# The last store of a group-norm kernel split by partitions: 120 rows, then 8 rows

## Chip, cores and metric

One core of one Trainium2 chip. The metric is the device time of one execution in microseconds (us). The profile's span is about 1.8 us shorter than this time. Runs are called fast when they are within 1.5% of the fastest of the same kernel.

## The reference

```python
B, C, H, W = 128, 1024, 32, 16          # bfloat16 in and out
xr = x.reshape(B, 32, C // 32, H, W)    # 32 groups
mu  = xr.mean(axis=(2, 3, 4), keepdims=True)
var = ((xr - mu) ** 2).mean(axis=(2, 3, 4), keepdims=True)
xn  = ((xr - mu) / jnp.sqrt(var + 1e-5)).reshape(B, C, H, W)
return xn * g[None, :, None, None] + b[None, :, None, None]
```

134 MB are read and 134 MB written; the profile's DMA packets carry both, 268.7 MB in all.

## The kernel before

The batch is cut into NT = 64 tiles of 2 samples. A tile is 128 partitions by 8192 bfloat16 columns, so a row is 16 KB and a tile 2 MB. Loads and stores are all issued from one queue (SP), nine loads ahead. VectorE scales the tile in place, one instruction for each of 16 channels, and the tile is stored as one transfer.

```python
    def L(i):
        st = state.setdefault(i, {})
        xt = xpool.tile([P, F], BF16, name="xt")
        chain("sp", nc.sync.dma_start(out=xt[:], in_=x_v[i]))
        st["xt"] = xt
    ...                                  # statistics on TensorE, VectorE, ScalarE
    def A(i):
        ...                              # reciprocal, scl, bia
        for k in range(KC):              # KC = 16
            chain("dve", nc.vector.tensor_scalar(
                out=xt[:, k * HW : (k + 1) * HW], in0=xt[:, k * HW : (k + 1) * HW],
                scalar1=scl[:, k : k + 1], scalar2=bia[:, k : k + 1],
                op0=ALU.mult, op1=ALU.add))

    def S(i):
        st = state[i]
        chain("sp", nc.sync.dma_start(out=o_v[i], in_=st["xt"][:]))
        state.pop(i - 3, None)
    ...
    for s in range(-1, NT + 2):
        ...                              # M1, M, Gm, A(s - 2), R, Q, T
        if 0 <= s - 2 < NT:
            S(s - 2)
            if s - 2 + PREFETCH < NT:
                L(s - 2 + PREFETCH)
```

Of the kernel before, what the change touches and what calls it, by code (L numbers as in the profile page):

```python
# [24 lines left out]
def kernel(  # L25
# [7 lines left out]
    nc = tc.nc  # L33
    P = nc.NUM_PARTITIONS
# [5 lines left out]
    NT = B0 // NS  # L40
# [16 lines left out]
    o_v = out.rearrange("(t n) (cb k) h w -> t (n cb) (k h w)", n=NS, cb=CB)  # L57
# [19 lines left out]
    def chain(key, inst):  # L77
        prev = last.get(key)
        if prev is not None:
            tc.add_manual_dep(inst.ins, prev.ins.name, nosync, reason="pipeline order")  # L80
        last[key] = inst
        return inst
# [5 lines left out]
        out=ind_f[:].rearrange("p (a c) -> p a c", c=PPG),  # L88
        in_=ones_f[:].rearrange("p (a c) -> p a c", c=PPG),
# [7 lines left out]
        out=ind_f[:].rearrange("p (a c) -> p a c", c=PPG),  # L97
        in_=ind_f[:].rearrange("p (a c) -> p a c", c=PPG),
# [165 lines left out]

    def S(i):
        st = state[i]
        chain("sp", nc.sync.dma_start(out=o_v[i], in_=st["xt"][:]))
        state.pop(i - 3, None)

    for i in range(min(PREFETCH, NT)):  # L270
# [16 lines left out]
    for s in range(-1, NT + 2):  # L287
        if 0 <= s + 1 < NT:
            M1(s + 1)
            M(s + 1)  # L290
        if 0 <= s - 1 < NT:
            Gm(s - 1)
        if 0 <= s - 2 < NT:
            A(s - 2)
        if 0 <= s + 1 < NT:
            R(s + 1)
        if 0 <= s < NT:
            Q(s)
        if 0 <= s - 1 < NT:
            T(s - 1)  # L300
# [4 lines that stand above are left out]
# [30 lines left out]
```

## Time and profile before

| | before |
|---|---|
| time, median of 4 | 639.52 us (639.23 to 639.78) |
| span in the profile | 637.8 us |
| moved | 268.7 MB, 421 GB/s over the span |
| last scaling by VectorE ends, last store issued | 621.0 us |
| wait for that store at the end | 15.4 us |

The kernel is bound by its transfers: the DMA engines move 421 GB/s over the span. The page of the kernel before, first its 40 slices of the span (the busy share of the DMA engines in tenths, and GB/s), then its DMA queues (packets, MB, share of the time of 16 engines):

```profile
DMA  8999999999999999999999999999999999999993
GB/s 357 427 427 426 428 425 429 434 428 423 434 429 429 430 431 432 430 431 430 432 429 431 432 431 431 428 431 433 431 429 430 432 432 430 429 432 431 430 423 163
...
q1 hardware_dynamic: 18752, 268.45, 98.7%
q8 instruction: 7, 0.11, 0.1%
q14 instruction: 15, 0.12, 0.0%
```

The engines are 9 tenths busy or more in all slices but the first and the last. The page calls the queues q8 and q14 instruction queues, so their packets are called instruction fetches here: few packets.

The end of the span in stretches of 2 us (columns: stretch, length, busy time and number of instructions of each compute engine, clock granted to TensorE, mean busy share of the 16 DMA engines, GB/s):

```profile
622.00:624.00 2.00, 0.00 (x0) 0.00 (x0) 0.00 (x0) 0.00 (x0) 0.00 (x0) 0.50 0.98 418
624.00:626.00 2.00, 0.00 (x0) 0.00 (x0) 0.00 (x0) 0.00 (x0) 0.00 (x0) 0.50 0.98 418
626.00:628.00 2.00, 0.00 (x0) 0.00 (x0) 0.00 (x0) 0.00 (x0) 0.00 (x0) 0.50 0.63 270
628.00:630.00 2.00, 0.00 (x0) 0.00 (x0) 0.00 (x0) 0.00 (x0) 0.00 (x0) 0.50 0.15 66
630.00:632.00 2.00, 0.00 (x0) 0.00 (x0) 0.00 (x0) 0.00 (x0) 0.00 (x0) 0.50 0.08 33
632.00:634.00 2.00, 0.00 (x0) 0.00 (x0) 0.00 (x0) 0.00 (x0) 0.00 (x0) 0.50 0.08 33
634.00:636.00 2.00, 0.00 (x0) 0.00 (x0) 0.00 (x0) 0.00 (x0) 0.00 (x0) 0.50 0.06 25
636.00:638.00 2.00, 0.00 (x0) 0.00 (x0) 0.00 (x0) 0.00 (x0) 0.00 (x0) 0.50 0.00 0
```

Up to 626 us all engines are at work. From 628 on a share of 0.15, then 0.08, is left: 0.08 of 16 engines is 1.3 engines. For some eight microseconds only one to three engines work. The waits of the SP queue (line, what it waited for, us in total, times, longest) show the final wait:

```profile
SPq L330 <- DMA out_dram<-xt: 15.4, 1, 15.4
```

The records of single packets in the trace say more. Each engine moves its eight rows of a store one after another, 0.611 us for each 16 KB row, then a 4-byte packet of 9 ns, taken here for its count: the queue q1 has 2112 of them, as many as the trace has landings. The stream that ends last has its rows of the store before the last one done at 631.56 us and those of the last store at 636.42. The others end at 630.90, 629.41, 628.61 and from there down to 626.8. So the stream that ends last is alone for the last 5.5 us. The trace gives no engine's number to a packet. So "late stream" below means: the one that ends last.

The late stream does not fall behind at the end. Its landing trails the median landing of the same transfer by 0.4 us at the start and 9.1 us at the end. About 3 us of this had come by 150 us, less regularly; from there on the lag grows mostly in steps of 0.8 to 1 us, at the landings at 159, 218, 272, 326, 376, 430, 485, 544 and 598 us among others. Just before each of these a q14 packet starts (157.5, 213.5, 268.4, 324.5, 371.6, 427.2, 482.6, 538.2 and 596.2 us). It takes 0.31 us itself, and in eight of the nine places a row that starts right behind it takes 1.0 to 1.2 us instead of 0.61.

### The profile page before, as it was taken

How to read it: one execution, taken by the hardware profiler on the slowest of the kernel's cores; microseconds unless marked ns; L12 is line 12 of the kernel's file. 1: busy time of each engine (PE TensorE's matmuls, PEld its weight loads, DVE VectorE, ACT ScalarE, POOL GpSimd, SP SyncE). 2: the span in 40 equal slices, each digit the busy share in tenths (PEclk: the TensorE clock that was granted, in tenths of full speed). 3: DMA queues.
4: the chain of work that ended last, by engine and by line, in shares of the span. 5: the costliest groups of instructions: out<-in, count | busy, mean ns of one | idle time of the engine just before them, and what ended most of it. 6: DMA issues, size and time to landing. Idle time of an engine off the chain costs nothing.

```text
span 637.8 us, 3899 instructions
## 1 busy us (share of the span) xinstructions
PE 326.3 (51%) x887; PEld 127.1 (20%) x904; DVE 421.0 (66%) x1349; ACT 590.7 (93%) x318; POOL 1.6 (0%) x6
## 2 busy tenths in 40 slices
PE   4654564556456555645654664464553654635300
PEld 1221122122112212211221222121221221212100
DVE  0086677668667766866776686677667667767680
ACT  1999999999999999999999999999999999999920
POOL 1000000000000000000000000000000000000000
PEclk9767767776776676666667667766766667666655
DMA  8999999999999999999999999999999999999993
GB/s 357 427 427 426 428 425 429 434 428 423 434 429 429 430 431 432 430 431 430 432 429 431 432 431 431 428 431 433 431 429 430 432 432 430 429 432 431 430 423 163
DMA packets 18774, 268.69 MB, mean 421 GB/s; under 512 B 2368, under 2 KB 2368, under 8 KB 2368
## 3 DMA queue, kind: packets, MB, share of 16 engines
q1 hardware_dynamic: 18752, 268.45, 98.7%
q8 instruction: 7, 0.11, 0.1%
q14 instruction: 15, 0.12, 0.0%
HBM read 134.23 MB, written 134.22 MB: 421 GB/s over the span
## 4 chain that ended last, share of the span: by engine, by line
ACT 53%; DMA 23%; issue 17%; DVE 2%; PE 1%; SPq 0%; DVEq 0%; ACTq 0%
ACT ja L189 38%; DMA out_dram<-xt 18%; ACT ja L137 14%; DMA xt<-in_x_dram 5%; DVE xt L255 2%; ACT rstd L221 1%; PE ps L154 1%; SPq L121 0%; DVE jd L171 0%; DVE bia L243 0%; DVE scl L237 0%; DVEq L330 0%; DVE rstd L232 0%; ACTq L137 0%
## 5 line engine op out<-in xcount | busy, mean ns | idle before, releaser
L189 ACT ACTIVATE ja<-xt,negmean 128x8192 bf16<-128x8192 bf16 x64 | 455.8, 7122 | 15.2 <-DVE jd L171 13.2
L154 PE MATMUL ps<-xt,ind_b 128*128 128x512 bf16 x759 | 301.9, 576 | 80.3 <-DMA xt<-in_x_dram 73.1
L255 DVE TENSOR_SCALAR xt<-xt,scl,bia 128x512 bf16<-128x512 bf16 x1024 | 336.6, 408 | 2.6 <-DVE bia L243 0.2
L154 PEld LDWEIGHTS <-ind_b 128*128 128x128 bf16 x776 | 108.6, 146 | 244.8 <-issue 162.4
L232 DVE RECIPROCAL rstd<-rstd 128x1 f32<-128x1 f32 x64 | 10.5, 164 | 169.1 <-ACT rstd L221 169.1
L137 ACT ACTIVATE ja<-xt 128x2048 bf16<-128x2048 bf16 x62 | 117.7, 1898 | 2.6 <-DMA xt<-in_x_dram 2.6
L243 DVE SCALAR_TENSOR_TENSOR bia<-scl,negmean,bet 128x16 f32<-128x16 f32 x64 | 15.0, 235 | 2.3
L237 DVE TENSOR_SCALAR scl<-gam,rstd 128x16 f32<-128x16 f32 x64 | 15.0, 234 | 2.2
L189 ACT ACTIVATION_READ_ACCUMULATOR ja<-xt,negmean 128x1 f32 x64 | 11.9, 186 | 0.0
L137 ACT ACTIVATION_READ_ACCUMULATOR ja<-xt 128x1 f32 x62 | 11.7, 189 | 0.0
L171 DVE TENSOR_SCALAR_CACHE_REDUCE jd<-ps 128x512 bf16<-128x512 f32 x2 | 1.4, 692 | 7.9 <-PE ps L154 7.9
L171 DVE TENSOR_SCALAR_CACHE_REDUCE jd<-ps,ps_170 128x512 bf16<-128x512 f32 x1 | 0.8, 755 | 6.6 <-PE ps_170 L206 6.6
L284 DVE CAST gam<-gam_b 128x16 f32<-128x16 bf16 x1 | 0.2, 174 | 6.4 <-DMA gam_b<-in_g_dram 6.4
L206 PE MATMUL ps_3186<-carry,ind_f 128*128 128x1 f32 x2 | 0.6, 362 | 6.7 <-ACT ja L189 6.7
L206 PE MATMUL ps_2155<-carry,ind_f 128*128 128x2 f32 x2 | 0.6, 362 | 4.8 <-ACT ja L137 4.8
L206 PE MATMUL ps_930<-carry,ind_f 128*128 128x2 f32 x2 | 0.6, 364 | 4.8 <-ACT ja L137 4.8
L206 PE MATMUL ps_1812<-carry,ind_f 128*128 128x2 f32 x2 | 0.6, 364 | 4.7 <-ACT ja L137 4.7
L206 PE MATMUL ps_587<-carry,ind_f 128*128 128x2 f32 x2 | 0.6, 364 | 4.7 <-ACT ja L137 4.7
L206 PE MATMUL ps_1469<-carry,ind_f 128*128 128x2 f32 x2 | 0.6, 362 | 4.6 <-ACT ja L137 4.6
L206 PE MATMUL ps_244<-carry,ind_f 128*128 128x2 f32 x2 | 0.6, 364 | 4.6 <-ACT ja L137 4.6
L206 PE MATMUL ps_1126<-carry,ind_f 128*128 128x2 f32 x2 | 0.6, 364 | 4.6 <-ACT ja L137 4.6
L206 PE MATMUL ps_2008<-carry,ind_f 128*128 128x2 f32 x2 | 0.6, 362 | 4.6 <-ACT ja L137 4.6
(319 smaller groups left out, 126.9 us busy)
## 6 DMA issues: line engine op xcount, KB each, us to landing
xt<-in_x_dram SPq DMA_DIRECT2D x64, 2048.0 KB, 24.2
out_dram<-xt SPq DMA_DIRECT2D x64, 2048.0 KB, 28.7
gam_b<-in_g_dram SPq DMA_DIRECT2D x2, 2.0 KB, 7.1
bet_b<-in_b_dram SPq DMA_DIRECT2D x2, 2.0 KB, 6.7
```

The source lines that it names most:

```text
L137: nc.scalar.activation(out=ja[:, 0 : na * MMN], in_=xt[:, (NMM - na) * MMN :], func=ACT.Identity, scale=-inv_n, accum_out=carry[:, 1:2],),
L154: nc.tensor.matmul(out=ps[:], lhsT=ind_b[:], rhs=xt[:, k * MMN : (k + 1) * MMN], start=(k == 0), stop=(k == npe - 1),),
L171: nc.vector.tensor_scalar(out=jd[:], in0=st["ps"][:], scalar1=-inv_n, scalar2=seed, op0=ALU.mult, op1=ALU.add, accum_out=negmean[:],),
L189: nc.scalar.activation(out=ja[:], in_=st["xt"][:], func=ACT.Square, bias=st["negmean"][:], scale=1.0, accum_out=carry[:, 0:1],),
L206: nc.tensor.matmul(out=ps2[:, 0:ncol], lhsT=ind_f[:], rhs=st["carry"][:, 0:ncol], start=True, stop=True,),
L221: nc.scalar.activation(out=rstd[:], in_=st["ps2"][:, 0:1], func=ACT.Sqrt, bias=eps_t[:], scale=inv_n),
L232: chain("dve", nc.vector.reciprocal(out=rstd[:], in_=rstd[:]))
L237: nc.vector.tensor_scalar(out=scl[:], in0=gam[:], scalar1=rstd[:], scalar2=None, op0=ALU.mult),
L243: nc.vector.scalar_tensor_tensor(out=bia[:], in0=scl[:], scalar=negmean[:], in1=bet[:], op0=ALU.mult, op1=ALU.add,),
L255: nc.vector.tensor_scalar(out=xt[:, k * HW : (k + 1) * HW], in0=xt[:, k * HW : (k + 1) * HW], scalar1=scl[:, k : k + 1], scalar2=bia[:, k ...
L284: nc.vector.tensor_copy(out=gam[:], in_=gam_b[:])
```

## The change

The intent is to take the last store off one DMA engine. In the trace of before, a store of 128 rows has sixteen landings, one for each stream with its eight rows. I expected 120 rows to go to fifteen engines, eight each, and the eight rows left to eight engines. One engine, the sixteenth, then has nothing to do in the last store.

```diff
     def S(i):
         st = state[i]
-        chain("sp", nc.sync.dma_start(out=o_v[i], in_=st["xt"][:]))
+        xt = st["xt"]
+        if i == NT - 1:
+            lo = P - P // 16
+            chain("sp", nc.sync.dma_start(out=o_v[i][0:lo, :], in_=xt[0:lo, :]))
+            chain("sp", nc.sync.dma_start(out=o_v[i][lo:P, :], in_=xt[lo:P, :]))
+        else:
+            chain("sp", nc.sync.dma_start(out=o_v[i], in_=xt[:]))
         state.pop(i - 3, None)
```

No other instruction moves on any engine.

## The prediction

Passages are cut from the recorded text where no trace or run shows what they say: how rows are dealt out to numbered engines, why the late engine should be 15 (the "about 80%" was my estimate, from nothing in the traces), a conclusion from the times of the fetches, and a term of the sum for rows of the last store that slow each other. "Engine 15" is my name for the engine that 120 rows leave out, "0 to 7" for those that also get one of the last 8 rows; "port contention" is my name for rows that slow each other. The sum came to about 634.6 us if the emptied engine is the late one (4.8 us less), and to 639.5 to 640.1 us if another is; the term for port contention, a guess of mine, put the time at about 637 us in the first case; weighed, 635.3 us.

> **What bounds the kernel now.** Data movement. The page shows the 16 DMA engines busy 9 tenths in nearly every slice at about 430 GB/s, 268 MB in 637.8 us. ScalarE is 93% busy but is fed by loads, and the chain of waits alternates between landings and ScalarE. The change touches only the last store, so only the tail counts.
>
> **The tail.** The last VectorE scaling ends at 621.0 us (timeline) and the last store is issued at 621.04; the span ends at 637.8. The waits show the final wait for that store: 15.4 us. The windows view shows the drain: DMA share 0.98 for 622-626 us, 0.63 for 626-628, 0.15 for 628-630, then 0.08, 0.08 and 0.06 up to 636. 0.08 of 16 engines is 1.3 engines. So 2 MB needs about 5 us on most engines, then one engine works alone for some 7 us. In the trace's packets a 16 KB row takes 0.611 us; the stream that ends last finishes the previous store at 631.56 us, then moves its eight rows of the last store, done at 636.42. The second-last stream ends at 630.90, the third at 629.41, most others between 626.0 and 628.6. The last stream's lag behind the median grows by 0.8 to 1 us at the times of 8 KB instruction fetches, about every 55 us[...]. The trace does not number the engines.
>
> **What the change does.** [...] Added: one issue on the queue (0.33 to 0.42 us in the trace, hidden under the drain) and one more row on eight engines, 0.61 us. Removed: 8 x 0.611 = 4.9 us from engine 15. [...]
>
> **Sum, if the late engine is 15 (about 80%).** It ends at 631.56 instead of 636.42. The second-last, plus one row, ends at 631.5. The span shrinks by 4.8 us, all on the critical path: about 634.6 us. [...] If the late engine is not 15, nothing is gained and up to 0.6 us lost: 639.5 to 640.1. Weighing these: 635.3 us.
>
> **What would show it.** Right: unchanged until 621 us; the stream late by 5 us ends at 631.6 with no rows of the last store; DMA share near 0.1 for 628-631.6, then nothing; final wait about 10.5 us. Port contention: packets of about 1.2 us after 622, none before. Wrong engine: one stream still ending at 636.4 or 637.0.
>
> **What would make it wrong.** Another engine being late, port contention, 120 rows spread otherwise than over fifteen engines, or a run-to-run drift of the fetches. In any case the stake is under 1% of the time.

## The result

| | before | after |
|---|---|---|
| time, median (4 runs each) | 639.52 us | 643.29 us (642.89 to 643.67) |
| ratio of fast runs | | 1.0061, 95% interval 1.0047 to 1.0075 |
| span in the profile | 637.8 us | 641.1 us |
| rows moved after 621 us that took over 0.9 us | 0 of 178 | 53 of 179, median of these 1.22 us |

The kernel became 3.8 us slower. That is 0.6%; the interval leaves out 1. Ratios are the mean time of one kernel's fast runs over that of the other's of the same rounds, so not quite the ratio of the medians quoted. The page after the change, the slices of the span again, and its DMA issues (KB each, us to landing; the transfer of 128 KB has no landing time there):

```profile
DMA  9999999999999999999999999999999999999993
GB/s 359 425 427 423 422 432 424 428 431 428 430 433 429 432 430 427 435 429 428 432 430 434 430 426 432 431 430 432 429 430 432 429 432 432 428 431 430 431 408 96
...
out_dram<-xt SPq DMA_DIRECT2D x63, 2048.0 KB, 28.7
out_dram<-xt SPq DMA_DIRECT2D x1, 1920.0 KB, 18.9
out_dram<-xt SPq DMA_DIRECT2D x1, 128.0 KB
```

All slices but the last two are as before, within 10 GB/s. The stretches at the end, to be read against those of before:

```profile
622.00:624.00 2.00, 0.00 (x0) 0.00 (x0) 0.00 (x0) 0.00 (x0) 0.00 (x0) 0.50 1.06 344
624.00:626.00 2.00, 0.00 (x0) 0.00 (x0) 0.00 (x0) 0.00 (x0) 0.00 (x0) 0.50 0.85 262
626.00:628.00 2.00, 0.00 (x0) 0.00 (x0) 0.00 (x0) 0.00 (x0) 0.00 (x0) 0.50 0.96 279
628.00:630.00 2.00, 0.00 (x0) 0.00 (x0) 0.00 (x0) 0.00 (x0) 0.00 (x0) 0.50 0.60 164
630.00:632.00 2.00, 0.00 (x0) 0.00 (x0) 0.00 (x0) 0.00 (x0) 0.00 (x0) 0.50 0.26 82
632.00:634.00 2.00, 0.00 (x0) 0.00 (x0) 0.00 (x0) 0.00 (x0) 0.00 (x0) 0.50 0.18 57
634.00:636.00 2.00, 0.00 (x0) 0.00 (x0) 0.00 (x0) 0.00 (x0) 0.00 (x0) 0.50 0.08 33
636.00:638.00 2.00, 0.00 (x0) 0.00 (x0) 0.00 (x0) 0.00 (x0) 0.00 (x0) 0.50 0.06 25
638.00:640.00 2.00, 0.00 (x0) 0.00 (x0) 0.00 (x0) 0.00 (x0) 0.00 (x0) 0.50 0.04 16
640.00:642.00 2.00, 0.00 (x0) 0.00 (x0) 0.00 (x0) 0.00 (x0) 0.00 (x0) 0.50 0.02 4
```

Read the last two columns together. Before, a busy share of 0.98 moved 418 GB/s. Now 0.96 (626 to 628 us) moves 279 GB/s: the engines are as busy, but rows take longer (53 of 179 over 0.9 us). That is the collision that the prediction priced as a risk. And the end of the list is not shorter than before: the share of 0.06 and 0.08 of the one late engine still stands there, up to 640 us. The final wait confirms it:

```profile
SPq L336 <- DMA out_dram<-xt: 18.7, 2, 18.1
```

What the late stream did, from the landings of its part of each transfer (us from the start of the span, the last landing of each transfer):

| | before: landing, since the one before | after: landing, since the one before |
|---|---|---|
| store 61 | 627.04 | 626.42 |
| store 62 (the one before the last) | 631.90, 4.86 | 634.39, 7.97 |
| last store, or its 120 rows | 636.75, 4.85 | 639.29, 4.90 |
| its last 8 rows | | 639.90, 0.61 |

Two things are seen at once. First, the trace has fifteen landings of the 120 rows and eight of the last 8, as meant, but the late stream still has eight rows of the 120 and one of the last 8, so it is not the engine that the change empties; it is one of the eight that got a ninth row. Second, most of the loss is not in the last store at all: the late stream's rows of the store before it took 7.97 us instead of 4.86. The sum is 3.11 + 0.05 + 0.61 = 3.77 us, and the difference of the medians is 3.77 us too (643.29 less 639.52). That even the last digit agrees is chance, for the landings are those of one execution each. The spans differ by only 3.3 us since in the profiled run of after the late stream happened to be 0.6 us earlier already at store 61.

### The profile page after: what moved, and what is told of

The parts are those of the page before. It is cut to its first block, busy times and chain, and to the rows that moved or that the text cites. A ratio compares the mean times of both kernels' runs of the same rounds, so it can differ in the third digit from the quotient of the medians.

```text
span 641.1 us, 3917 instructions
## 1 busy us (share of the span) xinstructions
PE 333.1 (52%) x904; PEld 127.4 (20%) x904; DVE 420.7 (66%) x1349; ACT 590.6 (92%) x318; POOL 1.6 (0%) x6
## 4 chain that ended last, share of the span: by engine, by line
ACT 56%; DMA 19%; issue 19%; DVE 2%; PE 1%; SPq 0%; DVEq 0%; ACTq 0%
ACT ja L189 41%; ACT ja L137 15%; DMA out_dram<-xt 14%; DMA xt<-in_x_dram 5%; DVE xt L255 2%; ACT rstd L221 1%; PE ps L154 1%; SPq L121 0%; DVE jd L171 0%; DVE scl L237 0%; DVE bia L243 0%; DVE rstd L232 0%; DVEq L336 0%; ACTq L137 0%
## 5 line engine op out<-in xcount | busy, mean ns | idle before, releaser
L154 PE MATMUL ps<-xt,ind_b 128*128 128x512 bf16 x776 | 307.7, 580 | 66.1 <-DMA xt<-in_x_dram 66.1
```

Of the source, the lines that this page charges most:

```text
L154: nc.tensor.matmul(out=ps[:], lhsT=ind_b[:], rhs=xt[:, k * MMN : (k + 1) * MMN], start=(k == 0), stop=(k == npe - 1),),
```

## The experiments

Sixteen kernels ran. The edits are to S(i) for the last tile, if nothing else is said. The theories:

- **Rows side by side** (the "port theory" of the expectations; the name is mine, and no run here shows a port). Rows of partitions that lie side by side slow each other when several engines read them at the same time. Before, with sixteen engines on 128 rows, no row of 178 took over 0.9 us; with 120 rows over fifteen engines, 53 of 179 did. e3, e4, e5 and e13 test the theory itself.
- **Rivals.** The HBM side of the new row order; the fewer engines or the second transfer as such; the ninth row alone.

### Which engine is late: a fingerprint (e1, e6), then a check (e7, e15)

A transfer of a few rows was expected to give one row each to as many engines; the trace of after has eight landings for its 8 rows. A series of small transfers of different sizes then leaves on each stream a number of small packets that tells in how many of them it took part. I numbered the streams by this, from 0: stream m is the one that takes part in the transfers of more than m rows (of 1 to 15). That the streams join in such a fixed order was my assumption; e10 and e15 test it at one place only.

```diff
+c = F - 256                      # e1
+chain("sp", nc.sync.dma_start(out=o_v[i][:, 0:c], in_=xt[:, 0:c]))
+lo = 0
+for k in [8] + list(range(15, 0, -1)):        # e6: (1, 2, 3, 4, 5, 6, 7, 100)
+    chain("sp", nc.sync.dma_start(out=o_v[i][lo : lo + k, c:F], in_=xt[lo : lo + k, c:F]))
+    lo += k
```

> The last store keeps all 128 rows and 7936 of 8192 columns in one transfer over sixteen engines; the last 256 columns go in sixteen small transfers of 8, 15, 14, ... 1 rows, whose packets are 512 B. [...] My prediction (late engine is 15): the last stream has 0 such packets. Theory now (it is one of 0 to 7, because after the change the last stream still moved a ninth row): 9 to 16; my bet is engine 7, 9 packets. Large packets stay at 0.61 us, for this transfer has all 128 partitions. Time within 1 us of before.

Measured: 643.80 us (2 runs; before 639.88), later than expected by 3 us. Only eight transfers were under way at a time, and the queue waited for the late stream before it issued the rest (three waits at the small transfers' line, 9.8 us in all). The late stream had seven small packets directly behind its large ones, the transfers of 8, 15, 14, 13, 12, 11 and 10 rows, all that were issued by then. So it takes part in the transfer of 8 rows (one of 0 to 7, and not 15), but nothing finer follows.

> The first fingerprint showed seven small packets at the tail of the late stream and six at that of the second, which only says that both are among engines 0 to 7: the queue stopped at eight transfers in flight. Now the last 256 columns go in transfers of 1, 2, ... 7 rows, then 100. [...] My bet: late engine 7, none; second, some of 0 to 6. Rival: the late engine is any other of 0 to 6, which shows in the number. Time within 1.5 us of e1 (643.8).

Measured: 642.28 us (one run). The end of the late stream in the packet records (start in us, ns, bytes), with the queue's transfers of 1 to 7 rows all issued by then:

```
636.591  592  15872     the last of its eight large pieces
637.180    9      4     its count
637.185   27    512
637.209    9      4
637.215   27    512
637.238    9      4
637.244   27    512
637.268    9      4
637.274   27    512
637.297    9      4     then nothing for 1 us
```

Four small packets: by the assumed order, those of the transfers of 4, 5, 6 and 7 rows. The late engine is 3 in this numbering. My bet on 7 was wrong too. The second-last stream had two, at a time when the transfers of 1 to 6 rows were issued: engine 4.

> The change with its last eight rows as seven over seven engines and one over one engine. If the late engine is 7, its stream ends after eight rows of the last store and time is 0.6 us under that of the change (about 642.7 us); if it is one of 0 to 6, the ninth row stays and the time is that of the change (643.3 us).

```diff
-for lo, hi in ((0, 120), (120, 128)):         # the change, written as a loop
+for lo, hi in ((0, 120), (120, 127), (127, 128)):
```

Measured: 643.53 us (4 runs; ratio to before 1.0062, interval 1.0047 to 1.0077), as the change. The late stream still had its ninth row (landings at 640.21 and 640.81 us, 0.60 us apart). Engine 7 is out, as e6 says.

> As e10, but 124 rows over four engines (0 to 3) instead of 123 over three. If the late engine is 3, its stream now has 31 pieces of 5.5 KB more (0.215 us each in e10) behind its 635.1 us: 641.8, time about 645 us. Rival (the fingerprint was misread and the late engine is another, or rows on the lowest engines do not go where I think): engines 0 to 3 end earlier than in e10, the late one is as in e10, time about 638.5 us.

Its edit, beside that of e10 (below), which gave the same columns to engines 0 to 2:

```diff
-for lo, hi in ((0, 123), (123, 126), (126, 128)):     # e10: 123 rows, k = 3
+for lo, hi in ((0, 124), (124, 128)):                 # e15: 124 rows, k = 4
```

Measured: 645.71 us (2 runs) against 638.52 us for e10. The late stream went on for 6.58 us behind its eight large pieces, which is 31 pieces of 0.212 us, a quarter of the 124 rows. In e10 the three small transfers have eight counts together (18888 packets in q1 against 18752 before, of which 128 are the pieces), as 3, 3 and 2 engines would give. One more engine for the same bytes costs seven microseconds, because the fourth is the late one. Two independent readings, the count of small packets and the time lost, agree. The numbers are those of the order above; the trace itself has none.

### What made the rows slow (e2, e3, e4, e5, e13)

> The last store as two transfers of 64 partitions, 16 engines each, so every engine still moves eight rows and none is left out; there is no ninth row. Port theory[...]: rows of the last store take about 1.2 us, the late stream is slowed by its neighbour on rows it has still to move, time 2 to 4 us over before. Rival (what costs is the transfer on fewer than sixteen engines and its ninth row): rows stay at 0.61 us, time within 0.5 us of before.

```diff
+for lo in (0, P // 2):
+    chain("sp", nc.sync.dma_start(out=o_v[i][lo : lo + P // 2, :], in_=xt[lo : lo + P // 2, :]))
```

Measured: 643.04 us (4 runs; ratio 1.0050, interval 1.0033 to 1.0067). As e2 is meant, no engine is left out and none has a ninth row, and still 73 of 176 rows take over 0.9 us and the late stream's rows of store 62 take 8.21 us, 3.35 more than before, which alone makes up the loss. So neither the missing engine nor the ninth row is the main cost. The ninth row costs 0.61 us of the 3.8 us of the change, as its landings above show; here 3.2 us are lost without it.

> The last store as sixteen transfers of 8 rows each, on eight engines, with rows 4 partitions apart[...]. Port theory: rows take 0.61 us; the late stream, if it is one of engines 0 to 7, has sixteen rows and ends near 631.6 + 9.8 = 641.4 us, time about 644.5 us. Rival (splitting or running on fewer engines is itself slow, or the HBM side): rows of 1.2 us or more, time 650 us or more.

> The same sixteen transfers of 8 rows on eight engines, but with 8 consecutive rows each[...]. Port theory:[...] 1.2 us or more in the median, time 648 to 664 us. Rival (number of transfers and engines decides, not the partitions): the same packets and time as with rows 4 apart.

```diff
+for lo in (0, 32, 64, 96):                     # e3: rows 4 apart
+    for j in range(4):
+        chain("sp", nc.sync.dma_start(out=o_v[i][lo + j : lo + j + 29 : 4, :],
+                                      in_=xt[lo + j : lo + j + 29 : 4, :]))
```
```diff
+for lo in range(0, P, 8):                      # e4: rows side by side
+    chain("sp", nc.sync.dma_start(out=o_v[i][lo : lo + 8, :], in_=xt[lo : lo + 8, :]))
```

Measured: e3 644.60 us, no row over 0.9 us of 176; e4 651.96 us, 87 of 180 rows over 0.9 us. Both have sixteen transfers of eight rows (eight landings for such a transfer in the trace of after) and the same bytes; what differs is which rows move at the same time, and so the partitions read and the HBM rows written together. e3 shows besides that many transfers on few engines do not slow rows by themselves. Two stretches of each, e3 first (columns as above):

```profile
634.00:636.00 2.00, 0.00 (x0) 0.00 (x0) 0.00 (x0) 0.00 (x0) 0.00 (x0) 0.50 0.37 152
636.00:638.00 2.00, 0.00 (x0) 0.00 (x0) 0.00 (x0) 0.00 (x0) 0.00 (x0) 0.50 0.47 197
```

```profile
634.00:636.00 2.00, 0.00 (x0) 0.00 (x0) 0.00 (x0) 0.00 (x0) 0.00 (x0) 0.50 0.10 41
636.00:638.00 2.00, 0.00 (x0) 0.00 (x0) 0.00 (x0) 0.00 (x0) 0.00 (x0) 0.50 0.57 90
```

In e3 a share of 0.47 moves 197 GB/s, in e4 a share of 0.57 moves 90 (636 to 638 us in both). e3 also gives the price of a row on the late engine without a collision: eight rows more than before, 4.7 us (644.60 less 639.88), 0.59 us each.

> Wrong result on purpose: sixteen transfers of 8 rows of the last tile, read from 8 consecutive partitions as in e4_eight_contig, but written to HBM rows 4 apart as in e3_eight_step4. Port theory (the SBUF side decides): as e4, time 650 to 654 us, many rows of over 0.9 us. Rival (the HBM addresses decide): as e3, rows of 0.61 us, time about 644.6 us.

> Wrong result on purpose, the mirror of e5: rows read from partitions 4 apart, written to eight consecutive HBM rows. Port theory: as e3, rows of 0.61 us, time about 644.6 us. HBM theory: as e4, about 652 us.

```diff
+for lo in range(0, P, 8):                      # e5; e13 has lo and d exchanged on the two sides
+    d = 32 * (lo // 32) + (lo % 32) // 8
+    chain("sp", nc.sync.dma_start(out=o_v[i][d : d + 29 : 4, :], in_=xt[lo : lo + 8, :]))
```

Measured: e5 651.34 us (80 of 175 rows slow), e13 644.14 us (0 of 175 slow). Rows that lie side by side in SBUF are slow here whether they go to neighbouring HBM rows (e4, 87 of 180) or not (e5, 80 of 175); none of the rows 4 apart is slow (e3, 0 of 176; e13, 0 of 175), whatever HBM rows they go to. The HBM side is out. (Both give wrong results.)

### Why the store before the last one suffered (e16, e17)

If collisions anywhere slowed every stream, it would not matter to the late stream which partitions its neighbours read. I expected it to matter ("own-port theory" in e17). e16 and e17 are e2 with both halves read from the same half of the tile, the upper in e16, the lower in e17.

```diff
+h = P // 2                                     # e16; e17: h = 0
+for lo in (0, P // 2):
+    chain("sp", nc.sync.dma_start(out=o_v[i][lo : lo + P // 2, :], in_=xt[h : h + P // 2, :]))
```

> Wrong result on purpose: e2 with both halves of the last store read from partitions 64 to 127. The rows of the last store still collide with each other (1.2 us and more). [...] its rows of the store before keep 0.61 us and eight of them take 4.9 us, not the 8.2 us of e2: time 639.5 to 640.5 us. Rival (collisions anywhere slow every stream): 8 us again, time 643 us.

> Wrong result on purpose, the mirror of e16: both halves read from partitions 0 to 63[...]. Own-port theory: the late stream's eight rows of the store before take as long as in e2 or longer (8 to 11 us), time 643 to 646 us. Rival (collisions anywhere slow every stream alike): same time as e16.

Measured, before in the same rounds 639.62 us (both give wrong results):

| | time (2 runs) | slow rows after 621 us | late stream's rows of store 62 |
|---|---|---|---|
| e16, partitions 64 to 127 twice | 640.51 us | 96 of 177 | 4.85 us |
| e17, partitions 0 to 63 twice | 644.56 us | 90 of 177 | 10.00 us |

Stretches of both, e16 first:

```profile
626.00:628.00 2.00, 0.00 (x0) 0.00 (x0) 0.00 (x0) 0.00 (x0) 0.00 (x0) 0.50 1.09 262
628.00:630.00 2.00, 0.00 (x0) 0.00 (x0) 0.00 (x0) 0.00 (x0) 0.00 (x0) 0.50 1.05 229
...
634.00:636.00 2.00, 0.00 (x0) 0.00 (x0) 0.00 (x0) 0.00 (x0) 0.00 (x0) 0.50 0.08 33
```

```profile
626.00:628.00 2.00, 0.00 (x0) 0.00 (x0) 0.00 (x0) 0.00 (x0) 0.00 (x0) 0.50 1.00 213
628.00:630.00 2.00, 0.00 (x0) 0.00 (x0) 0.00 (x0) 0.00 (x0) 0.00 (x0) 0.50 0.93 188
...
634.00:636.00 2.00, 0.00 (x0) 0.00 (x0) 0.00 (x0) 0.00 (x0) 0.00 (x0) 0.50 0.17 25
```

Between 626 and 630 both collide: about 1.0 of share and under 265 GB/s. But in e16 the late engine runs at its own pace through all this, and from 634 on it is alone at full speed (0.08 of share, 33 GB/s), as before the change. Nearly twice as many slow rows as in the change (96 against 53) cost almost nothing (640.51 us), because they are not the late stream's rows. In e17 its rows take twice their time. So the late stream is slowed by neighbours that read partitions 0 to 63 (10.00 us for eight rows) and not by those that read 64 to 127 (4.85 us), and what the collisions do to other streams is hidden under its lag. Two more traces narrow this down. In e4, where its neighbours read rows side by side, its rows of store 62 took 7.80 us (landings at 627.73 and 635.53 us). In e3, with rows 4 apart, they took 4.85 us (627.15 and 632.00), although its neighbours also read from the lower half at the time. The test in e3 is thin, for only seven rows of neighbours fall on these eight rows; which partitions the late stream itself reads, no trace shows.

### Where the lag comes from (e9, e11)

> Wrong result on purpose: VectorE scales two channels at a time with the first one's factors, 8 instructions per tile instead of 16; the last store is that of before. If the late engine is late because it also serves VectorE's instruction fetches (each 8 KB fetch of the long series adds 0.8 to 1 us of lag, 10 or 11 of them before), there are 6 or 7 fetches in that series, the lag of the last landing behind the median falls from 9.1 us to about 5.5 us, and the time falls by about 3.5 us, to 636 us. Rival (the lag has another cause, the fetches only coincide): lag and time stay.

```diff
-        for k in range(KC):                    # in A(i), every tile
+        for k in range(0, KC, 2):
             ...
-                    out=xt[:, k * HW : (k + 1) * HW],   # in0 likewise
+                    out=xt[:, k * HW : (k + 2) * HW],
```

Measured: 636.19 us (4 runs; ratio 0.9947, interval 0.9930 to 0.9964), a wrong result. The lag of the last landing is 5.9 us instead of 9.1, and q14 has 12 packets instead of 15. VectorE's scaling before and in e9 (group of instructions, count, busy us, mean ns):

```profile
L255 DVE TENSOR_SCALAR xt<-xt,scl,bia 128x512 bf16<-128x512 bf16 x1024 | 336.6, 408 | 2.6 <-DVE bia L243 0.2
```

```profile
L255 DVE TENSOR_SCALAR xt<-xt,scl,bia 128x1024 bf16<-128x1024 bf16 x512 | 239.4, 542 | 2.6 <-DVE bia L243 0.3
```

VectorE itself was not the limit: its last scaling ends at 621 us before, almost 16 us before the last landing. Its faster scaling does not explain the gain either, for the median landing of the last store stayed (627.68 us before, 627.50 in e9); only the late stream's came earlier. What fell with the lag is the number of its instructions: the regular series of 8 KB fetches has 11 members before (VectorE runs 1349 instructions) and 7 in e9 (837 instructions). Four fetches fewer went with 3.2 us less lag; which engine carries them, the trace does not say.

> Correct result; the last store is that of before. GpSimd scales five of the sixteen channels of each tile, so VectorE runs 320 of its 1349 instructions less. If the lag comes from VectorE's instruction fetches, the long series has 2 or 3 fetches fewer, the lag of the last landing falls by 2 to 2.5 us, and the time by as much, to about 637.3 us, unless GpSimd's own fetches land on the same engine or its scaling holds VectorE up so long that stores start late (then no gain or a loss of several us).

```diff
-            chain("dve", nc.vector.tensor_scalar(
+            onpool = k >= KC - 5               # in A(i), every tile
+            chain("pool" if onpool else "dve",
+                  (nc.gpsimd if onpool else nc.vector).tensor_scalar(
```

Measured: 637.32 us (5 runs; ratio 0.9961, interval 0.9950 to 0.9973), correct. The lag at the end is 6.5 us, and the median landing of the last store again stayed (627.98 us). q14 has 18 packets, more than before, and GpSimd now runs 326 instructions instead of 6; the regular series has 9 (VectorE runs 1029 instructions). So it is not the count of all fetches that matters. Nor can the 2.5 us be told off fetch by fetch: those of the series near 192 and 260 us left no step in the lag, and why is open. This version beats both kernels, by 2.5 us (before in the same rounds: 639.80) and, across jobs, by 6 us. The final wait shows the same:

```profile
SPq L331 <- DMA out_dram<-xt: 13.4, 1, 13.4
```

A price is visible: VectorE's scaling takes 596 ns instead of 408 beside GpSimd's (818 ns each). It is hidden under the transfers here.

### Taking bytes off engine 3 (e10, e12, e14)

> The second fingerprint names engine 3 as the late one and engine 4 as the second, so work for engines 0 to 2 alone is work taken off both: the last store keeps 5376 of 8192 columns for all 128 rows on sixteen engines, and the other 2816 columns of 126 rows go in transfers of 123 and 3 rows on three engines (two rows on two). Engine theory (a late engine ends later by what it moves itself): engine 3 moves eight pieces of 10.75 KB instead of 16 KB, 1.7 us less, and ends near 634.8, time 1.6 us under before. Port theory[...]:[...] time within 0.5 us of before.

```diff
+c = 5376
+chain("sp", nc.sync.dma_start(out=o_v[i][:, 0:c], in_=xt[:, 0:c]))
+for lo, hi in ((0, 123), (123, 126), (126, 128)):
+    chain("sp", nc.sync.dma_start(out=o_v[i][lo:hi, c:F], in_=xt[lo:hi, c:F]))
```

Measured: 638.52 us (5 runs; ratio 0.9977, interval 0.9964 to 0.9990), correct. This is the intent of the change, carried out on the engine that is late, and it gains 1.3 to 1.5 us. Here the simple engine theory was nearly right (1.6 us) and my port theory was wrong (no gain): the late stream's rows of store 62 took 4.85 us, unslowed, although the small transfers, which read all 128 partitions between them, were under way beside it (a DMA share of 0.24 to 0.35 from 626 to 634 us). The small pieces were slowed instead: 15 of 128 took 0.25 to 0.52 us where the others took 0.215. Why pieces of 5.5 KB give way and whole rows do not, no run here shows.

> Correct result; the last store is that of before. The split of e10 (2816 columns over engines 0 to 2) is made at the last load instead, which engine 3 works off while it alternates loads and stores, some 9 us behind the others. [...] engine 3 is spared 1.7 us and nothing is given back: time 1.7 us under before, about 637.9 us. [...]

The same four transfers in L(i) for the last tile. Measured: 638.78 us median (638.41 to 640.71, 6 runs; ratio 0.9988, interval 0.9977 to 1.0000). In the profiled run the last landing came at 635.44 us instead of 636.75, but two of the six runs were slower than 639.5. The interval allows a gain of 0 to 1.5 us: less than the expected 1.7, and whether loads and stores slow each other stays open.

> Correct result: e11 (GpSimd scales five of sixteen channels) with the last store split as in e10, here with 6016 columns on sixteen engines and 2176 over engines 0 to 2. If the two gains have separate causes (less lag from fetches; fewer bytes left on engine 3), they add: e11's 637.3 us less 0.27 of 4.9 us, about 636.0 us. If one takes away the room of the other, 637 us or more.

Measured: 637.44 us (5 runs; ratio 0.9965, interval 0.9951 to 0.9979), no better than e11 alone. The two do not add. In its trace the pieces on engines 0 to 2 land last, at 634.3 to 634.8 us, where e11's last landing was at 634.5; and two of the late stream's pieces took 1.02 and 0.54 us instead of 0.45. With less lag the three engines had no spare time left to give.

## Why the prediction was wrong

- **What bounds the end: right.** One stream ends 5.5 us after all others, and most of its 9.1 us of lag came with instruction fetches (nine steps of 0.8 to 1 us). e9 and e11 made the lag smaller by taking VectorE's instructions away, by 3.2 us and 2.5 us.
- **"If the late engine is 15 (about 80%)": the step that failed.** The late engine is 3 (e6, e15). Nothing in the profile said 15. The number came from the change itself, which empties the engine called 15, and from a belief about slow engines that no trace here shows; the late engine takes part in 8-row transfers (after, e1), so it is another. The gain of 4.8 us went with this step: the late stream kept its eight rows and got a ninth.
- **"If the late engine is not 15, nothing is gained and up to 0.6 us lost": mis-sized.** The ninth row was right, 0.61 us. The missing term is the 3.11 us by which the late stream's rows of the store before were slowed. I had thought of the collision, but only beside an emptied late engine, as something that delays the streams of the last store. I did not ask whose rows were still waiting when the last store began. It was the late stream: when the last store was issued at 621 us, it had all of stores 61 and 62 still to move (its part of store 61 landed at 627.04). With this term the sum is 3.77 us, as measured.
- **Collision of 120 rows: right in kind.** Rows of about 1.2 us (median 1.22 us) appear after 621 us, none before, as named. e3, e4, e5 and e13 put it on the SBUF side and on the partitions that are read at the same time.
- **The range.** The largest time in the text, 640.1 us, is the wrong-engine branch without the collision; the collision was priced only beside an emptied late engine. Two risks that were each named separately came together.

## What to carry to other kernels

The last store here ended with its slowest stream, 5.5 us after the others, so look at the drain after the last transfer before touching it: a busy share near 1/16 (0.06 to 0.08 here) means one engine's backlog, and moving work between engines helps only if you know which engine it is: a series of small transfers of 1, 2, ... rows named it in one run here (e6), up to the assumed order, and e10 and e15 checked it (638.52 against 645.71 us). And splitting a tile by consecutive partitions made engines collide on the SBUF side here and slowed rows of an *earlier* transfer still under way (7.97 us instead of 4.86 for the late stream's eight rows); a transfer that is cut by columns and keeps all 128 partitions ran at full speed (no large piece over 0.9 us in e1 and e10).
